# Strided sparse attention with a multiplicative FFN: batch 0's strided V issued from ScalarE's queue

## The chip, the cores and the metric

The kernel runs on one core of one Trainium2 chip. A core has a matrix engine (TensorE, PE in the profile), three engines for elementwise work (VectorE, DVE; ScalarE, ACT; GpSimd, POOL) and SyncE (SP), which here only issues DMA transfers. Each engine works off its own list of instructions in order and waits for others by semaphores. A DMA transfer is issued by an engine's instruction and carried out by the core's 16 DMA engines. The metric is the device time of one execution in microseconds (us).

## What is computed

Attention over 8 batches of 8 heads, 576 tokens and head dimension 64, in which the first four heads see the last 32 tokens only and the other four see every 32nd token, followed by a feed-forward network whose two first products are multiplied with each other.

```python
def _attn_ref(q, k, v):
    B, H, S, D = q.shape                      # 8, 8, 576, 64
    stride = 32
    scores = 1.0 / np.sqrt(D) * np.matmul(q, k.transpose(0, 1, 3, 2))
    rel = pos[:, None] - pos[None, :]
    mask_local = (rel >= 0) & (rel < stride)
    mask_strided = (rel >= 0) & (pos[None, :] % stride == pos[:, None] % stride)
    ...
    attn = softmax(np.where(masks, scores, -1e9))
    return np.matmul(attn, v)

def _moe_ref(x, w1, w2, w3, w_out):           # 4608 tokens, 512, 1024
    return ((x @ w1) * (x @ w2) @ w3) @ w_out
```

## The kernel before

Scores are computed for pairs of heads, four pairs a batch: pairs 0 and 1 (heads 0 to 3) are local, pairs 2 and 3 (heads 4 to 7) strided. For each pair PE transposes q and k, multiplies them, ScalarE takes the exponential, PE multiplies by V, VectorE divides by the sum, PE transposes the result into `xT`, and from there the feed-forward products follow (`ab_parts`, lines 632 to 684). The products w3 and w_out are folded into one matrix on the way (`fold_tr`, `fold_mm`).

Batches 0 and 1 have a scheme of their own (the functions named `ah_...`, lines 393 to 553). Batch 0 is what the core does while the weights are still coming, and its order on PE is written out by hand in `stream` (lines 832 to 884): every PE instruction is kept in the order in which the program emits it (`pe`, line 75). The first three units of `stream` are `ah_Ti(p0, 0)` (transposes of q for pair 0, and a ScalarE copy into `qT`), `both(p0)` (the mask's bias into PSUM) and `ah_Ti(p0, 1)` (the same for k, with a VectorE copy into `kT`). The fourth is `ah_R(0)`, which transposes q and k of the last 64 tokens and copies them into `qT` (ScalarE) and `kT` (VectorE), line 438.

Loads are emitted first, in lines 929 to 945, and all are issued by SyncE in that order: q and k of heads 0 to 3 (`load_qk(0, 0)`), the last 64 tokens of both (`load_rest`), q and k of heads 4 to 7 (`load_qk(0, 1)`), local V in four transfers of 96 x 6 pieces of 256 bytes (`load_vL`, line 231), strided V in two (`load_vN`, lines 238 and 240: 512 KB in pieces of 1,024 bytes and 64 KB in pieces of 256), eight transfers for w1 and w2 (`load_w12`, line 190), then w3, w_out and batch 1. Each lands as float32 in a staging tile, of which there are nine in a ring (`stgp`, line 64), and is cast to float16, mostly by GpSimd (the helper at line 91). The first batch's tiles fill the ring exactly, so the first weight tile waits for the cast of the first q, and so on round the ring; the seventh and eighth weights and the first w3 take the places of the second local V and of the two of strided V.

GpSimd's order at the start is: masks, cast of q (heads 0 to 3), cast of q and k (heads 4 to 7), then for each pair of local V a cast (line 232) and a copy that shifts rows (line 233), then two casts and a small one for strided V (lines 242 and 244), then the weights.

`behind(ins)` (line 80) puts the instructions emitted in its block behind `ins` on the same engine, without a semaphore. `setup` is a dictionary of such instructions. Where nothing of the kind is said, the tool that builds the program chooses an engine's order from the order of emission.

Of the kernel before, what the change touches and what calls it, by code (L numbers as in the profile page):

```python
# [14 lines left out]
def _ap(t: bass.AP, off_add, dims):  # L15
    return bass.AP(tensor=t.tensor, offset=t.offset + off_add, ap=dims)
# [3 lines left out]
def kernel(  # L20
# [11 lines left out]
    nc = tc.nc  # L32
    B, H, S, D = q.shape
# [3 lines left out]
    P = 128  # L37
# [10 lines left out]
    LQ, LT = 96, 6  # L48
    XW, XN, YW = 126, 4, 72
    XC = XW * XN  # L50
    NM = 512
# [8 lines left out]
    NW, NC, NQ = 144, 4, 640  # L60
# [14 lines left out]
    def pe(ins):  # L75
        return tc.keep_in_program_order(ins)

    setup = {}

    def behind(ins):  # L80
        return tc.issue_after(ins.ins) if ins is not None else nullcontext()
# [4 lines left out]
    def copy(eng, out, in_):  # L86
        if eng == "a":
            return nc.scalar.copy(out=out, in_=in_)  # L88
        elif eng == "v":
            return nc.vector.tensor_copy(out=out, in_=in_)  # L90
        return nc.gpsimd.tensor_copy(out=out, in_=in_)  # L91
# [25 lines left out]
    for m, lo, n, w in ((8, 208, 18, P), (32, 352, 2, 64), (7, 0, 18, XW), (4, P, 18, YW)):  # L117
        sel = tmp[0:m, NW + lo:NW + lo + n * m]
        nc.vector.tensor_copy(out=sel.rearrange("r (t a) -> r t a", a=m),
                              in_=_ap(id16, 0, [[id16.ap[0][0], m], [0, n], [1, m]]))  # L120
        pe(nc.tensor.matmul(mps[0:w, lo:lo + n * m], sel[:, 0:w], sel, start=True, stop=True))
    for i in range(1, LT):
# [7 lines left out]
                          in_=_ap(maskN, 0, [[maskN.ap[0][0], P], [0, NC - 1], [1, NW]]))  # L130
    nc.vector.tensor_copy(out=idw[:, P:2 * P - 32], in_=id16[:, 0:P - 32])
    biasL = tmp[:, S:2 * S]
    for bias, mask in ((biasL, maskL), (biasN, maskN)):
# [5 lines left out]
                                       in_=_ap(maskX, 0, [[maskX.ap[0][0], XW], [0, XN - 1], [1, XW]]))  # L139
# [44 lines left out]
    def load_w12(g):  # L184
        cs = bass.ds(g * 512, 512)
        for wd, wh in ((moe_w1, w1h), (moe_w2, w2h)):
            src = wd.rearrange("(c p) n -> p c n", p=P)
            for c in range(0, KM, 2):
                st = stgp.tile([P, 2, 512], FP32, tag="stg")
                nc.sync.dma_start(st, src[:, c:c + 2, cs])  # L190
                copy("p", wh[:, c:c + 2, cs], st)
# [4 lines left out]
    def load(b, out, in_):  # L196
        ins = nc.sync.dma_start(out, in_)  # L197
        if b > AHEAD + 1:
            pe(ins)


    def load_qk(b, grp, engs="pp"):
        for nm, ten, eng in (("q", q, engs[0]), ("k", k, engs[1])):
            st = stgp.tile([P, 4, 4, D], FP32, tag="stg")
            load(b, st.rearrange("p h c d -> p h (c d)"),
                 ten[b, 4 * grp:4 * grp + 4, 0:NM].rearrange("h (p c) d -> p h (c d)", c=4))
            t = qkp.tile([P, 4, 4, D], FP16, tag=f"{nm}{grp}")
            with behind(setup["p"] if b == 0 and grp == 0 else None):
                ins = copy(eng, t, st.rearrange("p h c d -> p c h d"))
            if b == 1:  # L210
                pe(ins)
            x16[(b, nm, grp)] = t
# [12 lines left out]
    def load_vL(b, hps=(0, 1)):  # L225
        vt = v16L[b % 2]
        for hp in hps:
            hs = slice(2 * hp, 2 * hp + 2)
            st = stgp.tile([P, 2, LT, D], FP32, tag="stg")
            for h in range(2):  # L230
                load(b, st[0:LQ, h], v[b, 2 * hp + h].rearrange("(t p) d -> p t d", p=LQ))
            nc.gpsimd.tensor_copy(out=vt[0:LQ, hs, :, 0:D], in_=st[0:LQ])  # L232
            copy("p", vt[LQ:P, hs, 0:LT - 1, 0:D], vt[0:32, hs, 1:LT, 0:D])

    def load_vN(b):
        vt = v16X[b % 2]
        st = stgp.tile([P, 4, 4 * D], FP32, tag="stg")
        nc.sync.dma_start(st, v[b, 4:8, 0:NM].rearrange("h (p c) d -> p h (c d)", c=4))
        sy = stgp.tile([64, 4, D], FP32, tag="stg", name="sy")
        nc.sync.dma_start(sy, v[b, 4:8, NM:S].rearrange("h r d -> r h d"))  # L240
        for hs in (slice(0, 2), slice(2, 4)):
            nc.gpsimd.tensor_copy(out=vt[:, hs, 0:NC, 0:D], in_=st[:, hs].rearrange("p h (c d) -> p h c d", c=4))
            if hs.start == 0:
                nc.gpsimd.tensor_copy(out=vt[0:64, :, NC, 0:D], in_=sy)

    def load_vX(b):
        vt = v16X[b % 2]
# [19 lines left out]
    for b in range(B):  # L267
        for hp in range(4):
            s = Pair()
# [133 lines left out]
    def ah_T1c(s, i, dst):  # L403
        t = (qT, kT)[i]
        eng = "av"[i]
        if s.local:
            copy(eng, t[:, s.hp, 0:NM].rearrange("x (p c) -> x p c", c=4),
                 dst.rearrange("x (c p) -> x p c", c=4))
        elif i:
            copy(eng, t[:, s.hp, 0:NM], dst)  # L410
        else:
            copy(eng, t[:, s.hp].rearrange("x (c w) -> x c w", w=NW)[:, :, 0:P],
                 dst.rearrange("x (c p) -> x c p", c=4))

    def ah_Ti(s, i):
        ah_T1c(s, i, ah_T1(s, i))

    def ah_T(s):
        if s.b:
            ps = psM.tile([P, 2, NM], FP16, tag="m", name="tps")  # L420
            pst = [ah_T1(s, i, ps[:, i]) for i in range(2)]
        else:
            pst = [ah_T1(s, i) for i in range(2)]
        for i in range(2):
            ah_T1c(s, i, pst[i])

    def ah_R(b):
        if b:
            ps = psB.tile([P, 2, NB], FP32, tag="big", name="rps").bitcast(FP16)[:, 0]
        else:  # L430
            ps = psM.tile([P, 1024], FP16, tag="m", name="rps")
        pvs = [ps[:, 256 * i:256 * i + 256].rearrange("x (g a w) -> x g a w", g=2, a=2) for i in range(2)]
        src = x16[(b, "r")]
        for g in range(4):
            pe(nc.tensor.transpose(pvs[g // 2][:, g % 2].rearrange("x a w -> x (a w)"),
                                   src[:, 2 * g:2 * g + 2].rearrange("p h d -> p (h d)"), id16))
        for i, t in enumerate((qT, kT)):
            copy("av"[i], t[:, 0:2, NM:S], pvs[0][:, :, i])
        copy("v", kT[:, 2:4, NM:S], pvs[1][:, :, 1])

        def tail():
            copy("a" if b else "v", qT[:, 2:4].rearrange("x g (c w) -> x g c w", w=NW)[:, :, :, P:NW],
                 pvs[1][:, :, 0].rearrange("x g (j c) -> x g c j", c=4))

        return tail
# [344 lines left out]
    stream = []  # L790
# [31 lines left out]
    def ah_Tw(s, i, n):  # L822
        ps = psF.tile([P, 2 * NM], FP16, tag="f", name="tps")
        ah_T1(s, i, ps[:, 0:NM])
        warm(ps, n)
        ah_T1c(s, i, ps[:, 0:NM])
# [7 lines left out]
    add(both, p0)  # L834
    add(ah_Ti, p0, 1)
    add(lambda: rest0.append(ah_R(0)))
    add(ah_S0, p0, (0,))
    add(ah_T, p1)
# [48 lines left out]
    for p, s in enumerate(pairs):  # L887
        b, i = divmod(p, 4)
# [18 lines left out]
    pos = [0]  # L907
# [22 lines left out]
    load_rest(0, "v")  # L930
    load_qk(0, 1)
    load_vL(0)
    load_vN(0)
    load_w12(0)
    load_w12(1)
# [6 lines left out]
    load_rest(1)  # L942
    load_qk(1, 1)
    load_vL(1)
    load_vN(1)

    while pos[0] < batch_end[0]:
# [32 lines left out]
    def scores(s):  # L980
        both(s)
        ah_S0(s, (0, 1))

    plan = ((15, ah_T, p4), (16, lambda: ah_R(1)()), (17, ah_T, p5), (17, ah_S, p4), (19, ah_S, p5),
            (20, ah_T, p6), (20, late_homes), (21, ah_PV, p4, 0), (22, scores, p6), (22, ah_T, p7), (22, ah_PV, p4, 1),
            (23, ah_PV, p5, 0), (24, scores, p7), (24, ah_PV, p5, 1), (24, ph_T2, p4), (25, ph_TS, None, p8),
            (26, ph_T2, p5), (26, ah_PV, p6, 0), (27, ah_PV, p6, 1))
    for i, u in enumerate(units[:-1], 1):
        u()
        for x in plan:  # L990
            if x[0] == i:
                x[1](*x[2:])
    load_vL(2)
    load_qk(2, 1)
    load_vX(2)
# [66 lines left out]
```

## Time and profile before

| | us |
|---|---|
| median of 3 runs | 271.12 (270.52 to 271.79) |
| profiled execution | 269.93 |
| its span, first to last instruction | 268.2 |
| PE busy | 257.8 |
| VectorE, ScalarE, GpSimd busy | 156.2, 140.3, 99.0 |
| DMA queue of SyncE, share of 16 engines over the span | 50.3% |

The profile is of one execution. Times in its views count from the start of the span. The page gives busy times and costly groups for the whole span; the timeline gives an engine's instructions in order (start, duration, engine, line, operation, tiles written and read, shapes, count, and in brackets the idle time before and what ended it); the windows give busy times and DMA rates of chosen stretches. A line such as L91 can be a helper's: the tiles tell which copy it is. `SPq` and `ACTq` mark issues by an engine's sequencer, which count as no busy time. How long a transfer takes from issue to landing stands in the DMA view.

DMA in stretches of the start (share of the 16 DMA engines' time, GB/s):

| us | share | GB/s |
|---|---|---|
| 8 to 9 | 1.08 | 372 |
| 9 to 10 | 1.23 | 301 |
| 10 to 11 | 0.89 | 204 |
| 11 to 12 | 0.94 | 154 |
| 12 to 13 | 0.71 | 129 |
| 13 to 14 | 1.07 | 369 |

### The profile page before, as it was taken

Reading aid. Unit: us, or ns where it says so; the run is one execution under the profiler, and the core shown is the slowest. Engines: PE = TensorE matmul, PEld = TensorE weight load, DVE = VectorE, ACT = ScalarE, POOL = GpSimd, SP = SyncE. Lnnn points to the kernel's source line nnn. Section 1 sums busy time; section 2 is a strip of 40 time slices with the busy share of each in tenths; the row PEclk is TensorE's granted clock in tenths of the full one; section 3 lists DMA queues with packets and bytes.
Section 4 is the critical chain, followed back from the end, with each engine's and each line's share of the span. In section 5 each row is a group of like instructions: output and inputs, shape, how many; then the busy total and the mean of one; then the engine's idle time right before and its main releaser. Section 6 shows DMA issues by size and latency. Waiting matters only on the chain.

```text
span 268.2 us, 6827 instructions
## 1 busy us (share of the span) xinstructions
PE 257.8 (96%) x2703; PEld 136.4 (51%) x2703; DVE 156.2 (58%) x373; ACT 140.3 (52%) x300; POOL 99.0 (37%) x119
## 2 busy tenths in 40 slices
PE   2999999999999999999999999999999999999993
PEld 1664464565555555555555555555555544444442
DVE  6573533555678766867776777667866752322420
ACT  1774334677566666555556465555466544324331
POOL 5576886778347206511840185038200000000000
PEclk9999999999999999999999999999999999999998
DMA  7999999988597569336923973397330022013013
GB/s 222 260 343 368 409 420 327 257 249 229 174 320 210 181 202 260 116 119 207 291 74 120 268 222 104 123 275 213 100 120 0 2 78 81 0 41 115 2 39 120
DMA packets 61101, 48.69 MB, mean 182 GB/s; under 512 B 31804, under 2 KB 52492, under 8 KB 61068
## 3 DMA queue, kind: packets, MB, share of 16 engines
q1 hardware_dynamic: 57036, 40.97, 50.3%
q10 hardware_dynamic: 4032, 7.28, 7.2%
q8 instruction: 21, 0.34, 0.5%
q14 instruction: 12, 0.10, 0.1%
HBM read 38.80 MB, written 9.44 MB: 180 GB/s over the span
## 4 chain that ended last, share of the span: by engine, by line
PE 85%; DMA 9%; SPq 3%; POOL 1%; issue 0%; ACT 0%; DVE 0%; POOLq 0%
PE ops L719 28%; PE bps L676 21%; PE aps L667 21%; DMA st<-in_moe_w_dram 8%; PE sps L389 3%; SPq L197 3%; PE t2a L586 2%; PE pt L301 2%; PE sps L352 2%; DMA st<-in_v_dram 2%; PE tps L399 1%; PE trp L777 1%; PE sps L480 1%; PE t L560 1%; PE ops L747 0%; PE rps L624 0%
## 5 line engine op out<-in xcount | busy, mean ns | idle before, releaser
L667 PE MATMUL aps<-xT,w1h 128*128 128x512 f16 (+1 forms) x288 | 73.5, 376 | 0.0
L676 PE MATMUL bps<-xT,w2h 128*128 128x512 f16 (+1 forms) x288 | 73.1, 376 | 0.0
L679 DVE TENSOR_TENSOR abt<-bps,asb 128x512 f16<-128x512 f32 (+1 forms) x72 | 48.5, 678 | 36.5 <-PE bps L676 35.0
L91 POOL CAST t<-st 128x1024 f16<-128x1024 f32 (+1 forms) x46 | 45.8, 1004 | 63.5 <-DMA st<-in_q_dram 43.3
L88 ACT COPY asb<-aps 128x512 f32<-128x512 f32 (+1 forms) x71 | 41.4, 584 | 51.2 <-PE aps L667 45.8
L719 PE MATMUL ops<-w,abt 128*128 128x512 f16 x280 | 67.1, 379 | 0.0
L676 PEld LDWEIGHTS <-w2h 128*128 128x128 f16 x288 | 27.1, 98 | 30.9 <-issue 0.7
L667 PEld LDWEIGHTS <-w1h 128*128 128x128 f16 x288 | 26.8, 98 | 28.6 <-issue 0.3
L719 PEld LDWEIGHTS <-abt 128*128 128x128 f16 x280 | 25.2, 98 | 26.2
L730 ACT COPY osb<-ops 128x512 f32<-128x512 f32 x35 | 21.0, 600 | 20.3 <-PE ops L719 19.9
L375 ACT ACTIVATE pte<-sps 128x1024 f16<-128x1024 f32 (+1 forms) x24 | 24.4, 1019 | 13.2 <-PE sps L352 12.8
L552 DVE TENSOR_TENSOR xqs<-sps,rcp 128x768 f16<-128x768 f32 (+1 forms) x24 | 21.4, 891 | 0.8
L364 DVE TENSOR_TENSOR ptm<-pte,maskE 128x1152 f16<-128x1152 f16 (+2 forms) x16 | 12.8, 801 | 7.1 <-ACT pte L375 6.7
L719 PE MATMUL ops<-woh,w3T 128*128 128x512 f16 x64 | 15.3, 380 | 0.0
L90 DVE COPY kT<-pt 128x512 f16<-128x512 f16 (+4 forms) x28 | 11.4, 417 | 6.5 <-ACT kT L88 4.8
L88 ACT COPY qT<-pt 128x224 f16<-128x224 f16 (+4 forms) x40 | 14.9, 422 | 0.2 <-PE pt L309 0.2
L364 DVE TENSOR_TENSOR ptm<-pte,maskX 126x1152 f16<-126x1152 f16 x12 | 10.4, 869 | 7.7 <-ACT pte L375 7.7
L232 POOL CAST v16L<-st 96x768 f16<-96x768 f32 x16 | 13.4, 836 | 3.4 <-DMA st<-in_v_dram 1.8
L260 POOL CAST v16X<-st 126x1024 f16<-126x1024 f32 x6 | 6.9, 1151 | 19.7 <-DMA st<-in_v_dram 19.7
L389 PEld LDWEIGHTS <-ptm 128*128 128x128 f16 (+1 forms) x264 | 11.1, 98 | 5.8 <-DVE ptm L364 0.8
L90 DVE COPY xT<-t2a 128x384 f16<-128x384 f16 (+1 forms) x22 | 8.5, 388 | 7.7 <-PE t2a L586 7.3
L91 POOL COPY v16L<-v16L 32x640 f16<-32x640 f16 x16 | 12.3, 768 | 1.0
(124 smaller groups left out, 274.8 us busy)
## 6 DMA issues: line engine op xcount, KB each, us to landing
st<-in_q_dram SPq DMA_DIRECT2D x16, 512.0 KB, 4.4
st<-in_k_dram SPq DMA_DIRECT2D x16, 512.0 KB, 5.5
st<-in_moe_w_dram SPq DMA_DIRECT2D x16, 512.0 KB, 10.0
out_dram<-osb ACTq DMA_DIRECT2D x27, 256.0 KB, 2.0
st<-in_v_dram SPq DMA_DIRECT2D x32, 144.0 KB
st<-in_v_dram SPq DMA_DIRECT2D x24, 112.0 KB, 2.5
st<-in_moe_w_out_dram SPq DMA_DIRECT2D x4, 512.0 KB, 11.0
out_dram<-osb SPq DMA_DIRECT2D x8, 256.0 KB, 3.9
```

Of the source, the lines that this page charges most:

```text
L88: return nc.scalar.copy(out=out, in_=in_)
L90: return nc.vector.tensor_copy(out=out, in_=in_)
L91: return nc.gpsimd.tensor_copy(out=out, in_=in_)
L364: nc.vector.tensor_mul(o.rearrange("p (a x) -> p a x", x=x), i.rearrange("p (a x) -> p a x", x=x), _ap(s.mask, lo, [[s.mask.ap[0][0], s.kr ...
L375: nc.scalar.activation(out=pv[0:kr, :, lo:hi], in_=src, func=AF.Exp, bias=0.0, scale=scale)
L389: pe(nc.tensor.matmul(s.ps[:, h, c * 65:c * 65 + 65], s.ptm[0:s.kr, c0:c0 + P], s.v[0:s.kr, 2 * (s.hp % 2) + h, c, :], start=True, stop=True))
L552: nc.vector.tensor_mul(s.xqs[0:w, c0:c0 + l].rearrange("p i h d -> p h i d"), xv[:, :, :, 0:D], _ap(rcp, 0, [[rcp.ap[0][0], w], [LT, 2], [ ...
L667: pe(nc.tensor.matmul(st["a"][:, 0:nt], w1h[:, ci, bass.ds(jc * P, P)], xT[ci][:, tok], start=(ci == 0), stop=(ci == KM - 1)))
L676: pe(nc.tensor.matmul(st["b"][:, 0:nt], w2h[:, ci, bass.ds(jc * P, P)], xT[ci][:, tok], start=(ci == 0), stop=(ci == KM - 1)))
L679: nc.vector.tensor_mul(abts[tch][:, jc, skip:], st["b"][:, 0:nt], st["asb"][:, 0:nt])
L719: pe(nc.tensor.matmul(st["ps"], lhs(ci), rhs(ci), start=(ci == 0), stop=(ci == KF - 1)))
L730: nc.scalar.copy(out=osb, in_=ps)
```

## The change

Batch 0's two transfers of strided V are issued by ScalarE, behind its first copy of q (`setup["q"]`, set where that copy is made), and no longer by SyncE behind local V. ScalarE's copy of q for the last 64 tokens is put behind the second of them (`setup["y"]`). GpSimd's three casts of strided V are put behind the last copy of local V (`setup["h", 0]`). So that the first copy of q exists when `load_vN(0)` is emitted, the first three units of `stream` are emitted ahead of it. Batch 1 stays as it was.

```diff
-            copy("p", vt[LQ:P, hs, 0:LT - 1, 0:D], vt[0:32, hs, 1:LT, 0:D])
+            setup["h", b] = copy("p", vt[LQ:P, hs, 0:LT - 1, 0:D], vt[0:32, hs, 1:LT, 0:D])
 
     def load_vN(b):
         vt = v16X[b % 2]
+        eng = nc.sync if b else nc.scalar
         st = stgp.tile([P, 4, 4 * D], FP32, tag="stg")
-        nc.sync.dma_start(st, v[b, 4:8, 0:NM].rearrange("h (p c) d -> p h (c d)", c=4))
         sy = stgp.tile([64, 4, D], FP32, tag="stg", name="sy")
-        nc.sync.dma_start(sy, v[b, 4:8, NM:S].rearrange("h r d -> r h d"))
+        with behind(None if b else setup["q"]):
+            eng.dma_start(st, v[b, 4:8, 0:NM].rearrange("h (p c) d -> p h (c d)", c=4))
+        with behind(None if b else setup["q"]):
+            setup.setdefault("y", eng.dma_start(sy, v[b, 4:8, NM:S].rearrange("h r d -> r h d")))
         for hs in (slice(0, 2), slice(2, 4)):
-            nc.gpsimd.tensor_copy(out=vt[:, hs, 0:NC, 0:D], in_=st[:, hs].rearrange("p h (c d) -> p h c d", c=4))
+            with behind(None if b else setup["h", b]):
+                nc.gpsimd.tensor_copy(out=vt[:, hs, 0:NC, 0:D], in_=st[:, hs].rearrange("p h (c d) -> p h c d", c=4))
             if hs.start == 0:
-                nc.gpsimd.tensor_copy(out=vt[0:64, :, NC, 0:D], in_=sy)
+                with behind(None if b else setup["h", b]):
+                    nc.gpsimd.tensor_copy(out=vt[0:64, :, NC, 0:D], in_=sy)
...
         if s.local:
-            copy(eng, t[:, s.hp, 0:NM].rearrange("x (p c) -> x p c", c=4),
-                 dst.rearrange("x (c p) -> x p c", c=4))
+            ins = copy(eng, t[:, s.hp, 0:NM].rearrange("x (p c) -> x p c", c=4),
+                       dst.rearrange("x (c p) -> x p c", c=4))
+            if i == 0:
+                setup.setdefault("q", ins)
...
         for i, t in enumerate((qT, kT)):
-            copy("av"[i], t[:, 0:2, NM:S], pvs[0][:, :, i])
+            with behind(None if i or b else setup["y"]):
+                copy("av"[i], t[:, 0:2, NM:S], pvs[0][:, :, i])
...
     load_vL(0)
+    while pos[0] < 3:
+        stream[pos[0]]()
+        pos[0] += 1
     load_vN(0)
     load_w12(0)
```

## The prediction

> **What bounds the kernel now.** I read the page first, for which engine carries the span and which chain ended last.
>
> ```profile
> span 268.2 us, 6827 instructions
> PE 257.8 (96%) x2703; PEld 136.4 (51%) x2703; DVE 156.2 (58%) x373; ACT 140.3 (52%) x300; POOL 99.0 (37%) x119
> ```
>
> TensorE is busy for 257.8 of 268.2 us. I then cut the span into stretches: from 20 us to 35 us PE is busy 15.0 of 15.0 us, from 35 to 40 us 4.94 of 5, from 60 to 200 us 139.9 of 140. So behind about 20 us PE only works off its list, and whatever the start loses or gains goes to the end almost undiminished. Only the stretch from 7 us (first scores) to 20 us can be changed by this edit, so I laid the engines' timelines of that stretch side by side. SyncE's queue first:
>
> ```profile
> 3.97 1.22 SPq L197 DMA_DIRECT2D st<-in_k_dram  x1
> 5.23 4.92 SPq L197 DMA_DIRECT2D st<-in_v_dram  x4
> 10.19 0.82 SPq L238 DMA_DIRECT2D st<-in_v_dram  x1
> 11.06 0.60 SPq L240 DMA_DIRECT2D sy<-in_v_dram  x1
> 11.77 5.21 SPq L190 DMA_DIRECT2D st<-in_moe_w_dram  x8
> ```
>
> Start and duration of each issue. The two that move are those at 10.19 and 11.06; in front of them are four of local V, behind them the weights. Now ScalarE, GpSimd and TensorE:
>
> ```profile
> 7.65 0.58 ACT L88 COPY qT<-tps 128x512 f16<-128x512 f16 x1
> 9.32 0.27 ACT L88 COPY qT<-rps 128x128 f16<-128x128 f16 x1 [1.09 <-PE rps L435]
> 9.83 0.70 ACT L505 ACTIVATE ptm<-sps 128x640 f16<-128x640 f32 x1 [0.24 <-PE sps L480]
> ```
>
> ```profile
> 9.51 1.04 POOL L91 CAST t<-st 128x1024 f16<-128x1024 f32 x1 [3.42 <-DMA st<-in_q_dram]
> 10.83 1.04 POOL L91 CAST t<-st 128x1024 f16<-128x1024 f32 x1 [0.28 <-DMA st<-in_k_dram]
> 11.98 0.83 POOL L232 CAST v16L<-st 96x768 f16<-96x768 f32 x1
> 16.44 0.40 POOL L244 CAST v16X<-sy 64x256 f16<-64x256 f32 x1
> 17.52 1.04 POOL L91 CAST w1h<-st 128x1024 f16<-128x1024 f32 x1 [0.68 <-DMA st<-in_moe_w_dram]
> ```
>
> ```profile
> 12.24 0.84 PE L399 MATMUL tps<-idw,t 128*128 128x128 f16 x12
> 14.33 0.54 PE L537 MATMUL xpl<-v16L,ptm 128*128 128x65 f16 x12
> ```
>
> The reader is to see three things. ScalarE has a hole of 1.09 us behind its first copy of q. GpSimd waits for the second k (heads 4 to 7), which lands late, and from then on works without a pause until the strided V is done at 16.84. TensorE takes that k at 12.24, 0.37 us after its cast ended at 11.87. The last view is DMA between 3.3 and 5.1 us, where the last figure is issue to landing:
>
> ```profile
> st<-in_q_dram SPq DMA_DIRECT2D x1, 512.0 KB, 6.2
> st<-in_k_dram SPq DMA_DIRECT2D x1, 512.0 KB, 6.8
> ```
>
> The second q landed at 9.45 and the second k at 10.77, so they are 1.32 us apart. By the completion records, 15 of the 16 DMA engines had finished that k at 10.02 and one at 10.77; the same one is last in every transfer of the start. This engine, not the mean, sets each landing.
>
> **The change, part by part.**
>
> (a) *SyncE loses two issues.* The first weight issue can move from 11.77 to 10.19, 1.58 us earlier. But it lands 5.7 us after its issue (17.47), behind everything older, and the slowest DMA engine gets no less work. Worth nothing as long as that engine has no hole; GpSimd takes all eight of these weights as they land (0.2 to 1.2 us idle before each), and PE reads the first at 18.70, after its cast ends at 18.57. If the weights did land earlier, PE's only visible wait behind 20 us that hangs on them is 0.06 us at 36.3 (the idle part of 35 to 40 us). Bounds -0.2 (all of the 230 ns by which the matmul at 36.36 starts behind its predecessor's pace) and 0; I take -0.06.
>
> (b) *ScalarE gains two issues between its copies at 7.65 and 9.32, and the second copy is put behind them.* What is queued behind: that copy (q of the last 64 tokens, heads 0 to 3), then the first exp at 9.83, and from there ScalarE is busy nearly without a hole until 13.9. No such load on ScalarE's queue is in the trace. Nearest rows: 0.45 us for the same shape of load from SyncE's empty queue (at 0.80), 0.34 us for ScalarE's own stores, 0.82 and 0.60 us for these very two from SyncE's loaded queue. So 0.9 to 1.5 us for both with their gaps. The room: ScalarE's sequencer is free between 7.66 (the copy started) and 8.23 (it ended); the copy at 9.32 may slip 0.24 us before it moves the exp, so the room ends at 9.56. 1.33 to 1.90 us. It fits except at the worst of both (8.23 + 1.5 = 9.75, 0.2 late). I take 0; bounds 0 and +0.2, and a blocked queue is a rival below.
>
> (c) *The transfers start earlier and share the DMA engines.* The first packet came 1.12 us after the issue at 0.80 and 1.49 us after that at 10.19 (11.68, by the packet records). So they now begin between 7.66 + 1.12 = 8.78 and 8.23 + 1.49 = 9.72, while the second k is still on the slowest engine (its last packet starts at 10.42). If the two queues take turns there, each remaining packet of k waits for one of V: between 9.72 and 10.42 that is 0.70 us; from 8.78 on it is all of V's large transfer, of the same shape as k and thus 1.32 us. Bounds for k: 0 if V's packets came behind, 1.32 if all come before. Taking turns is nearest to one queue serving equal parts, so I take the middle of 0.70 and 1.32, 1.0 us. The cast of k then ends at 12.87, and PE, which reads a cast 0.05 us after it ends, has 0.32 us of slack at 12.24: **+0.68 us on PE**.
> The Trainium skill, "DMA: Bandwidth & Descriptors", section "Issuing engines are not separate DMA queues", speaks against the change: transfers started by different engines run on the same 16 DMA engines and interleave, and a second issuer saves only its issue time. By that rule the sum is this same loss for k and nothing for the weights; without it V would be free.
>
> (d) *GpSimd's order is pinned behind the local V casts.* It is the order that the trace has (11.98 to 15.25 local, 15.32 to 16.84 strided), so 0. Local V also lands later on the slowest engine, by V's 1.32 us: its last part for the first cast landed at 11.85, now about 13.2. The cast at 11.98 moves by 1.2, and so does the unbroken row behind it: first local V complete 13.59 to 14.8 (PE wants it at 14.33 + 0.68 = 15.0), strided V 16.84 to 18.05 (PE wants the last part at about 17.75 + 0.68 = 18.4), first weights 18.57 to 19.15 (PE: 18.70 + 0.68 = 19.4). All three are covered by PE's own delay, by 0.2 to 0.3 us. If that cover is gone, it costs up to 0.3 more.
>
> (e) *Emission of three stream units moves ahead of the loads.* They hold PE, ScalarE and VectorE work whose neighbours on each engine stay; 0.
>
> Sum: -0.06 + 0 + 0.68 + 0 + 0 = +0.62, so the span goes from 268.2 to 268.8 us. The profiled execution took 269.93 us, 1.7 more than its span, and the median of the runs is 271.12; on that scale the forecast is **271.7 us**. A measurement of this kernel tells about 0.5% (1.36 us) from no change, so the likeliest case counts as "within".
>
> **Rivals.**
>
> *ScalarE is held by SyncE's issues (slower).* SyncE issues its last local V from 8.46 to 10.15, 1.69 us where an empty queue takes 0.5. If ScalarE's issues have to wait likewise, at 1.69 + 1.24 us (the slowest local V, the slowest `sy`) from 7.66 they end at 10.6; if they wait until SyncE has done, at 10.15 + 1.47 = 11.6. Then the copy of 9.32 is 1.3 to 2.3 late, less 0.24 of slack: +1.1 to +2.1, 272.7 in the middle. It decides as soon as the issues end after 9.56. Against it, in the window around 87 us:
>
> ```profile
> 86.37 1.87 SPq L197 DMA_DIRECT2D st<-in_v_dram  x3
> 87.57 0.38 ACTq L734 DMA_DIRECT2D out_dram<-osb  x1
> ```
>
> ScalarE's store was issued amid three of SyncE's and took 0.38 instead of 0.34 us. Those queues were not full, though. The Trainium skill, "Perfetto Trace Analysis", section "DMA Instruction — HWDGE (DVE, Sync)", has the descriptor generator locked for one issuer at a time; by that the 11.6 above would hold, which the row at 87.57 does not bear out.
>
> *PE falls back to its slow pace.* The 128x128 transposes took 314 ns until 10.4 us and 219 after, 107 and 56 ns apart; PE had been working since 7.0. The page's granted clock shows 1.0 throughout. If a hole of 0.7 us at 12.3 sends it back for such a 3.4 us, that costs up to 3.4 x (1 - 56/107) = 1.6, less the waits it has anyway (0.6 us around 15, by the starts of its matmuls): +0.9 to +1.6 on top of 0.62, 273.0. Against it: it waits 0.24 us for ScalarE at 15.56 already and stays fast.
>
> *Not slower.* Between 10 and 13 us DMA moved 204, 154 and 129 GB/s in three stretches of 1 us, against 372 between 8 and 9, with a DMA share down to 0.71. If V's packets fill that dip and k keeps its place, k is not late and (a) gives up to -0.2: 271.0. It needs the slowest engine to serve the older queue first; then (c) is 0 to 0.3 and vanishes in PE's slack.
>
> *The change does not do what it says:* ScalarE's issue gets through only when SyncE's would have, and nothing moves: 271.1.
>
> **Chances.** Forecast 0.40, ScalarE held 0.20, slow pace 0.12, not slower 0.23, nothing 0.05. Slower by over 0.5% (beyond 272.5): most of the second and third and the forecast's upper tail, 0.14 + 0.11 + 0.06 = 0.31. Faster by over 0.5% only by something unseen: 0.07. Range 270.3 (not slower, with the runs' own spread of 0.6 below) to 273.7 (slow pace with its spread); the forecast alone: 271.0 to 272.4.
>
> **What would show it.** Two ScalarE issues between 7.66 and 9.56, ending before the copy at 9.32 (b); GpSimd's cast of the second k at about 11.8 instead of 10.83 and PE's twelve transposes at about 12.9 (c); the local V cast near 13.2 and no wait of PE for it (d); the weights landing where they did (a). If k's cast stays at 10.83, (c) is wrong and the time is 271.0; if the copy of 9.32 starts at 10.5 or later, the held queue is right; transposes of 314 ns after 12 us would show the slow pace.

## The result, and the profile after

| | before | changed |
|---|---|---|
| median of 9 runs each, us | 271.30 (270.52 to 272.54) | 273.22 (272.09 to 274.88) |
| profiled execution, us | 269.93 | 272.69 |
| its span, us | 268.2 | 271.0 |

The changed kernel takes 1.0061 times as long, interval 1.0036 to 1.0086: slower by some 1.7 us. It lies inside the range of 270.3 to 273.7, 1.5 us above the forecast of 271.7.

First the head of the profile's page, then SyncE's and ScalarE's timelines (start, duration) of the changed kernel:

```profile
span 271.0 us, 6827 instructions
PE 259.6 (96%) x2703; PEld 137.2 (51%) x2703; DVE 157.1 (58%) x373; ACT 140.2 (52%) x300; POOL 98.4 (36%) x119
```

```profile
4.81 4.79 SPq L197 DMA_DIRECT2D st<-in_v_dram  x4
9.72 7.53 SPq L190 DMA_DIRECT2D st<-in_moe_w_dram  x8
```

```profile
6.13 1.04 ACT L88 CAST t<-st 128x1024 f16<-128x1024 f32 x1 [4.05 <-DMA st<-in_k_dram]
6.36 0.48 ACTq L241 DMA_DIRECT2D st<-in_v_dram  x1
7.09 0.58 ACT L88 COPY qT<-tps 128x512 f16<-128x512 f16 x1
7.24 0.71 ACTq L243 DMA_DIRECT2D sy<-in_v_dram  x1
8.58 0.27 ACT L88 COPY qT<-rps 128x128 f16<-128x128 f16 x1 [0.91 <-PE rps L442]
9.39 0.70 ACT L513 ACTIVATE ptm<-sps 128x640 f16<-128x640 f32 x1 [0.55 <-PE sps L488]
```

The two issues did move: they take 0.48 and 0.71 us and end at 7.95, and the pinned copy at 8.58 waits for PE's transposes, not for them. The weights start at 9.72 instead of 11.77. The moved transfers' packets came much later than their issues: the first at 9.82. The DMA view (packets, MB, share of 16 engines' time) has ScalarE's queue, q10, not at all from 8 to 9.8 us, and from 9.8 to 10.4 us beside SyncE's q1:

```profile
q1 hardware_dynamic: 1231, 0.60, 114.4%
```

```profile
q10 hardware_dynamic: 130, 0.13, 62.3%
q1 hardware_dynamic: 313, 0.08, 57.6%
```

Now GpSimd and PE:

```profile
8.48 1.04 POOL L91 CAST t<-st 128x1024 f16<-128x1024 f32 x1 [2.83 <-DMA st<-in_q_dram]
10.37 1.04 POOL L91 CAST t<-st 128x1024 f16<-128x1024 f32 x1 [0.85 <-DMA st<-in_k_dram]
...
14.23 0.82 POOL L232 CAST v16L<-st 96x768 f16<-96x768 f32 x1 [1.23 <-DMA st<-in_v_dram]
...
17.37 2.01 POOL L91 CAST w1h<-st 128x1024 f16<-128x1024 f32 x2
```

```profile
10.25 0.34 PE L488 MATMUL sps<-qT,kT 64*128 64x96 f16 x4
11.24 0.24 PE L488 MATMUL sps<-qT,kT 64*128 64x64 f16 x2 [0.64 <-DVE kT L90]
11.40 0.61 PE L404 MATMUL tps<-idw,t 128*128 128x128 f16 x4
11.80 0.63 PE L828 MATMUL tps<-idw 128*128 128x128 f16 x4
...
13.93 0.99 PE L404 MATMUL tps<-idw,t 128*128 128x128 f16 x12
```

The second k is cast at 10.37, 0.46 us *earlier* than before, and PE takes it only at 13.93, 2.5 us after its cast has ended. Instead PE stands still at 10.6 for 0.64 us, waiting for VectorE. The same place in the kernel before has no wait, and what follows runs faster there:

```profile
10.58 0.29 PE L480 MATMUL sps<-qT,kT 64*128 64x96 f16 x6
10.80 0.40 PE L399 MATMUL tps<-idw,t 128*128 128x128 f16 x4
11.03 0.39 PE L820 MATMUL tps<-idw 128*128 128x128 f16 x4
```

What VectorE does there, before and then changed:

```profile
9.62 0.35 DVE L90 COPY kT<-rps 128x128 f16<-128x128 f16 x2 [0.34 <-ACT qT L88]
9.89 0.28 DVE L90 COPY qT<-rps 128x128 f16<-128x128 f16 x1
10.68 0.69 DVE L90 COPY kT<-tps 128x512 f16<-128x512 f16 x1 [0.51 <-PE tps L399]
```

```profile
10.36 0.69 DVE L90 COPY kT<-tps 128x512 f16<-128x512 f16 x1 [1.51 <-PE tps L404]
10.96 0.35 DVE L90 COPY kT<-rps 128x128 f16<-128x128 f16 x2
11.23 0.28 DVE L90 COPY qT<-rps 128x128 f16<-128x128 f16 x1
```

The order is turned round. The copies of the last 64 tokens of k (`kT<-rps`) could run at about 8.9, when ScalarE's copy of 8.58 has ended, but now stand behind the copy of pair 1's k (`kT<-tps`), which waits 1.51 us for PE's transposes. PE needs the last 64 tokens for the two matmuls at 11.24.

Matching the two traces matmul by matmul gives where the span's 2.76 us went. The changed kernel is 0.43 us ahead at its first transposes (its first q landed earlier), still 0.33 ahead at 10.25, and 0.56 behind at 11.24: a step of 0.88 for the wait. By 13.93 it is 1.69 behind, another 1.12 without any wait: PE there works at another pace. The groups of PE's instructions (busy us, mean ns of one, idle) show it; these are the transposes of one source line, in the changed kernel from 11.4 to 13.9 us and in the kernel before in the like stretch, from 10.8 to 13.1:

```profile
L828 PE MATMUL tps<-idw 128*128 128x128 f16 x4 | 0.6, 314 | 0.0
```

```profile
L820 PE MATMUL tps<-idw 128*128 128x128 f16 x8 | 0.8, 219 | 0.0
```

At 314 ns each PE is at the slow pace that it had until 10.40 us in the kernel before; in the changed one it lasts until 14.29. These moments are the starts of the first clock record in each trace, and the spacing of the 128x128 matmuls changes there from 107 to 56 ns. From 20 to 36 us the distance is 1.76. At 36 us PE catches up 0.23 (a wait is gone) and at about 110 us 0.19, which leaves 1.34, and between 110 and 195 us the distance grows by another 1.38, which the section on the hardware takes up.

So there are two suspects, VectorE's order and the slow pace, and the question is what made each, and whether the transfers themselves cost anything.

### The profile page after: what moved, and what is told of

Same layout as the page of the kernel before. It is cut to its first block, busy times and chain, and to the rows that moved or that the text cites. A ratio compares the mean times of both kernels' runs of the same rounds, so it can differ in the third digit from the quotient of the medians.

```text
span 271.0 us, 6827 instructions
## 1 busy us (share of the span) xinstructions
PE 259.6 (96%) x2703; PEld 137.2 (51%) x2703; DVE 157.1 (58%) x373; ACT 140.2 (52%) x300; POOL 98.4 (36%) x119
## 4 chain that ended last, share of the span: by engine, by line
PE 90%; DVE 5%; ACT 3%; issue 1%; ACTq 0%; DVEq 0%
PE ops L727 28%; PE aps L675 22%; PE bps L684 21%; PE sps L394 3%; PE pt L306 2%; PE t2a L594 2%; PE tps L404 2%; PE sps L357 2%; DVE ptm L369 2%; PE sps L500 2%; PE sps L488 1%; ACT pte L380 1%; PE t L568 1%; DVE abt L687 1%; PE xpl L545 1%
## 5 line engine op out<-in xcount | busy, mean ns | idle before, releaser
L380 ACT ACTIVATE pte<-sps 128x1024 f16<-128x1024 f32 (+1 forms) x24 | 24.4, 1018 | 13.2 <-PE sps L357 12.8
L369 DVE TENSOR_TENSOR ptm<-pte,maskX 126x1152 f16<-126x1152 f16 x12 | 11.9, 994 | 7.6 <-ACT pte L380 7.6
L90 DVE COPY kT<-pt 128x512 f16<-128x512 f16 (+4 forms) x28 | 11.4, 417 | 6.3 <-ACT kT L88 4.6
L232 POOL CAST v16L<-st 96x768 f16<-96x768 f32 x16 | 13.2, 824 | 3.9 <-DMA st<-in_v_dram 3.2
```

The lines of the kernel that those rows point to most:

```text
L369: nc.vector.tensor_mul(o.rearrange("p (a x) -> p a x", x=x), i.rearrange("p (a x) -> p a x", x=x), _ap(s.mask, lo, [[s.mask.ap[0][0], s.kr ...
L380: nc.scalar.activation(out=pv[0:kr, :, lo:hi], in_=src, func=AF.Exp, bias=0.0, scale=scale)
```

## The experiments

All ratios are to the kernel before, run beside them on the same chip. e1 to e4 share one set of such runs (median 270.98), e5 to e8 a second (272.21), and e9 and e10 a third (271.87).

**e1: the changed kernel with VectorE's order put back.** VectorE's copy of pair 1's k is pinned behind the last 64 tokens' copy of k.

```diff
-            ins = copy(eng, t[:, s.hp, 0:NM].rearrange("x (p c) -> x p c", c=4),
-                       dst.rearrange("x (c p) -> x p c", c=4))
+            with behind(setup["r", 0] if i and s is pairs[1] else None):
+                ins = copy(eng, t[:, s.hp, 0:NM].rearrange("x (p c) -> x p c", c=4),
+                           dst.rearrange("x (c p) -> x p c", c=4))
...
-        copy("v", kT[:, 2:4, NM:S], pvs[1][:, :, 1])
+        setup["r", b] = copy("v", kT[:, 2:4, NM:S], pvs[1][:, :, 1])
```

> The changed kernel with one pin more: VectorE's copy of k for pair 1 is put behind its copies of k for the last 64 tokens, as in the kernel before. Theory O (the loss comes from VectorE's order, which makes PE wait 0.64 us at 11.2 us and keeps it at its slow pace for one stretch of 3.4 us more): PE's last two 64x64 score matmuls of pair 0 no longer wait, its 128x128 transposes are 56 ns apart from about 10.4 us, and the time is that of the kernel before within 0.3% (271.0 to 271.6), if anything 0.2 us less for the earlier weights. Rival C (the loss comes from the two queues sharing the DMA engines and from ScalarE's issues): 272.7 to 273.5, as the changed kernel.

Measured: 271.54 us, ratio 1.0016 (0.9990 to 1.0042); the loss can't be seen any more. PE's timeline:

```profile
10.44 0.39 PE L489 MATMUL sps<-qT,kT 64*128 64x96 f16 x6
10.76 0.61 PE L404 MATMUL tps<-idw,t 128*128 128x128 f16 x4
```

The wait is gone (six matmuls in a row, the next at 10.76), though the pace stays slow until 14.14 and not, as expected, until about 10.4.

**e2: the kernel before with VectorE's order spoilt, no transfer moved.**

```diff
         for i, t in enumerate((qT, kT)):
-            copy("av"[i], t[:, 0:2, NM:S], pvs[0][:, :, i])
-        copy("v", kT[:, 2:4, NM:S], pvs[1][:, :, 1])
+            if i == 0 or b:
+                copy("av"[i], t[:, 0:2, NM:S], pvs[0][:, :, i])
+        if b:
+            copy("v", kT[:, 2:4, NM:S], pvs[1][:, :, 1])
...
+            if b == 0:
+                with behind(setup["k1"]):
+                    copy("v", kT[:, 0:2, NM:S], pvs[0][:, :, 1])
+                    copy("v", kT[:, 2:4, NM:S], pvs[1][:, :, 1])
```

(`setup["k1"]` is the copy of pair 1's k, set where that copy is made; the last four lines stand in the function that ends `ah_R`'s work, emitted later.)

> The kernel before with VectorE's order alone changed: the copies of k for the last 64 tokens are emitted later and put behind the copy of k for pair 1; all loads are issued by SyncE as before. Theory O: slower by 1.2 to 2.2 us (272.5 to 273.5), with PE waiting for VectorE's copy at about 11 us and its transposes 107 ns apart until about 13.8 us. Rival C: as before within 0.3%.

Measured: 273.18 us, ratio 1.0054 (1.0026 to 1.0082). With every load still on SyncE, the same order on VectorE brings the same wait of PE and the whole loss. VectorE's timeline, then PE's line for the two matmuls that wait:

```profile
10.38 0.69 DVE L90 COPY kT<-tps 128x512 f16<-128x512 f16 x1 [1.52 <-PE tps L399]
10.98 0.35 DVE L90 COPY kT<-rps 128x128 f16<-128x128 f16 x2
```

```profile
11.25 0.24 PE L488 MATMUL sps<-qT,kT 64*128 64x64 f16 x2 [0.64 <-DVE kT L90]
```

**e3: the changed kernel with PE kept at work in the hole.** Six matmuls on the identity, whose result nobody reads, ahead of the six score matmuls of which the last two wait.

```diff
+    add(lambda: warm(psF.tile([P, 2 * NM], FP16, tag="f", name="wps"), 6))
     add(ah_S0, p0, (1,))
```

> The changed kernel with six 128x128 matmuls into a PSUM tile that nobody reads, in front of the second group of pair 0's scores, where PE then waits 0.64 us. VectorE's order stays. If the slow pace hangs on how busy PE was in the stretch before, PE now reaches its fast pace at about 10.4 to 11 us, and 0.9 to 1.2 us of the loss are gone (272.0 to 272.4), while the wait itself (0.6 to 0.9 us) stays. If the pace has nothing to do with the hole: 273.2 or up to 0.3 more.

Measured: 271.65 us, ratio 1.0027 (0.9996 to 1.0057), against 1.0061 for the changed kernel as it is; in the profiled execution the pace switched at 10.96 instead of 14.29. VectorE's order is still there, and so is the delay: the six take 0.75 us from 10.44 on, and PE still waits 0.18 us in front of the two. About half of the loss thus looks to be pace and not the wait, though the two intervals overlap.

**e4: the changed kernel without the pin on ScalarE's copy.**

```diff
-            with behind(None if i or b else setup["y"]):
-                copy("av"[i], t[:, 0:2, NM:S], pvs[0][:, :, i])
+            copy("av"[i], t[:, 0:2, NM:S], pvs[0][:, :, i])
```

> The changed kernel without the pin that puts ScalarE's copy of q for the last 64 tokens behind its second issue. VectorE's order is then that of the kernel before, and ScalarE issues behind that copy, some 1.5 us later than in the changed kernel. Theory O: the time of the kernel before within 0.3% (271.0 to 271.6) as long as the two issues (0.5 and 0.7 us) delay the first exp by less than 0.5 us; with the exp later by 0.7 to 1.0, up to 272. Rival C: the transfers still share the engines, 272.5 or more.

Measured: 271.35 us, ratio 1.0009 (0.9984 to 1.0034). VectorE's order is that of the kernel before: the last 64 tokens of k are copied at 8.89, pair 1's k at 10.37.

```profile
8.89 0.36 DVE L90 COPY kT<-rps 128x128 f16<-128x128 f16 x2
10.37 0.69 DVE L90 COPY kT<-tps 128x512 f16<-128x512 f16 x1 [0.93 <-PE tps L404]
```

This names the cause of the new order. VectorE's copies of the last 64 tokens wait for ScalarE's copy of them (the row at 9.62 of the kernel before); that copy was pinned behind ScalarE's second issue; and with this pin the tool that builds the program puts VectorE's copies in the other order. How it chooses is not shown. The transfers are still issued by ScalarE here, though later, at 8.60 and 9.08, and cost nothing that can be measured.

**e5: the kernel before, unchanged, profiled again**, because its first profile might have shown a lucky pace.

> The kernel before once more, for a second profile of it. If the moment at which PE goes from 107 to 56 ns between 128x128 transposes differs from execution to execution, it is not at 10.4 us again but somewhere between 10.4 and 14.2 (the mended kernel had 14.1, though PE waited no more there than in the kernel before). If it is fixed by PE's list, it is at 10.4 plus or minus 0.4.

Measured: 271.03 us in one run. PE's timeline:

```profile
10.23 0.39 PE L480 MATMUL sps<-qT,kT 64*128 64x96 f16 x6
10.56 0.61 PE L399 MATMUL tps<-idw,t 128*128 128x128 f16 x4
10.96 0.63 PE L820 MATMUL tps<-idw 128*128 128x128 f16 x4
```

The same program, the same order, no wait, and yet slow until 14.95 here and until 10.40 in its first profile; the spans are 269.3 and 268.2. So the moment of the switch belongs to the execution and not to the kernel alone, and the first profile of the kernel before is of a quick execution, by 1.1 us of span against this one. Against this second profile the changed kernel loses 0.84 us at the wait, but its fast pace begins 0.66 us sooner (14.29 against 14.95), and from 17 to 60 us it is only 0.13 us behind. A pair of profiles shows the wait; what the change costs can be told from the medians alone.

**e6, e7, e8: kept warm from the start.** 33 matmuls of 128x128 on the identity, in PE's idle time of the first 6.7 us, in the kernel before (e6), in e1's kernel (e7) and in the changed one (e8). This is meant to bring the fast pace forward and to leave VectorE's order as the difference between e8 and e7.

```diff
+    wps = psF.tile([P, 512], FP32, tag="f", name="wps")
+    def prewarm(n):
+        for _ in range(n):
+            pe(nc.tensor.matmul(wps[:, 0:P], id16, id16, start=True, stop=True))
+    prewarm(20)
     # the masks' matmuls
...
+    prewarm(10)
...
     add(ah_Ti, p0, 0)
+    add(prewarm, 3)
```

> The kernel before with 33 matmuls of 128x128 on the identity into a PSUM tile that nobody reads: 20 in front of the mask's first matmul, 10 behind its last, 3 behind pair 0's transposes of q, all where PE waits. If PE's pace follows how busy it was in the 3.4 us before, it is fast from 5 to 8.5 us on in every execution: 0.5 to 1.5 us faster than the kernel before (269.5 to 270.5), and the spread of the runs, 2 to 3.5 us so far, shrinks. If the pace is set otherwise: no change within 0.2%.

> The changed kernel with VectorE's order mended, and the same 33 matmuls. With the pace out of the way, what the move to ScalarE's queue is worth by itself is its distance from the prewarmed kernel before: 0 within 0.2% if k and local V land in time, 0.3 to 1.0 us slower if PE at full pace now waits for the second k or for local V (the mechanism of the prediction's part (c) and (d)), 0.2 us faster if the earlier weights count.

> The changed kernel as it is, with VectorE's order that makes PE wait, and the same 33 matmuls. Its distance from the mended prewarmed kernel is the price of the wait alone: 0.6 to 0.9 us. If the wait costs only through the pace, 0 to 0.2 us.

| | median, us | ratio to before | slow pace until, us |
|---|---|---|---|
| e6, before | 270.42 | 0.9944 (0.9913 to 0.9975) | 9.47 |
| e7, changed, order mended | 269.47 | 0.9912 (0.9882 to 0.9942) | 10.13 |
| e8, changed | 270.19 | 0.9935 (0.9912 to 0.9958) | 7.67 |

The fast pace came later than the expected 5 to 8.5 us in e6 and e7, and the spread of e6's runs (269.16 to 272.74 us) did not shrink. e8 is 0.72 us above e7 in the medians, within the expected 0.6 to 0.9 us for VectorE's order alone; but the two intervals overlap, so this price is an estimate. Nor is e8 slower than e6 (270.19 against 270.42). PE's timelines of e8 and of e7 at the place:

```profile
9.55 0.26 PE L496 MATMUL sps<-qT,kT 64*128 64x96 f16 x4
10.53 0.20 PE L496 MATMUL sps<-qT,kT 64*128 64x64 f16 x2 [0.73 <-DVE kT L90]
10.67 0.40 PE L412 MATMUL tps<-idw,t 128*128 128x128 f16 x4
```

```profile
1.54 2.31 PE L121 MATMUL wps<-idw 128*128 128x128 f16 x20 [1.54 <-POOL idw masks.py:199]
...
10.39 0.40 PE L412 MATMUL tps<-idw,t 128*128 128x128 f16 x4
...
16.40 0.53 PE L554 MATMUL xpl<-v16L,ptm 128*128 128x65 f16 x12 [0.21 <-POOL v16L L91]
...
18.97 0.61 PE L684 MATMUL aps<-xT,w1h 128*128 128x512 f16 x2 [0.22 <-POOL w1h L91]
```

e7 has no wait at 10.39 but two small ones later, for local V and for the first weights, which land late and which a later PE would have covered. In this profiled pair the wait sets e8 back by 0.89 us against e7, yet at 20 us e8 is 0.39 us ahead, because e7 was slow for longer (10.13 against 7.67) and has its own two waits; so the pair does not confirm the 0.72. By its median e7 is the fastest kernel here. Against e6 its distance is 0.95 us, with intervals that overlap; in the profiled pair it doesn't come from the start, where e7 is 0.57 us *behind* e6 at 18.97, but for the most part from a wait of e6 for VectorE at 85 us (0.62). That moving the transfers is worth something at full pace is therefore indicated and not shown. Without the added matmuls nothing of it is to be seen (e1 and e10).

**e9, e10: the changed kernel and e1's kernel again, beside each other**, with no edit, because e1's distance to the changed kernel came from two sets of runs.

> The changed kernel once more, beside the mended one on the same chip. Slower than the kernel before by 0.4 to 0.8% as in its own runs; in the profile PE waits 0.64 us at 10.6 us as in the first one (the order is fixed), and becomes fast between 12 and 15 us (not fixed).

> The changed kernel with VectorE's order mended, once more. If the order is all of the loss, it is the kernel before within 0.25%, and faster than the changed kernel beside it by 0.3 to 0.6% (0.7 us of wait and up to 0.9 us of slow pace). If the queues have a share, it is slower than the kernel before by over 0.3%.

Measured: 272.83 us, ratio 1.0036 (1.0008 to 1.0065), and 271.30 us, ratio 0.9983 (0.9953 to 1.0012), so 1.53 us apart on one chip. e9's profile has the same wait once more:

```profile
11.95 0.23 PE L488 MATMUL sps<-qT,kT 64*128 64x64 f16 x2 [0.64 <-DVE kT L90]
```

It stayed slow until 17.38 (12 to 15 was expected), and e10 until 13.15. Beside the profile of the changed kernel, which is slow through the same stretch, e10 starts the four transposes behind the place of the wait at 10.58 instead of 11.40: 0.82 us for the wait at the slow pace. If 0.72 of the 1.53 us are the price of the order at full pace (e8 less e7, an estimate), some 0.8 are left for the pace. e3's step from 1.0061 to 1.0027, 0.9 us, is of the same size. How the loss divides between the two is thus indicated and not shown; that the order brings all of it on is shown by e1, e2, e4 and this pair.

## Why the prediction was right in time and wrong in its mechanism

The forecast was +0.6 us from a late k; the result is about +1.7 us, and PE waits for no k. That the time lies in the range is luck: 273.2 is beyond the 272.4 that the forecast alone reached, in the part of the range that stood for rivals, and the wait of PE that did come, for VectorE, was in none of them.

- **(a), SyncE's lost issues: right as to the issues.** The weights were issued 2 us earlier, and the first of them was cast at 17.37 instead of 17.52, now without a wait. PE's wait near 36.36 is gone, 0.23 us: the bound of -0.2, not the -0.06 taken. That the earlier weights did this is not shown, for e5, the kernel before again, has no such wait either: its PE arrives there at 37.77, 0.93 us after the cast has ended.
- **(b), ScalarE's issues at 0: right for the issues.** They started at 6.36 and 7.24, earlier than the 7.66 from which I counted: the first even before the copy that it stands behind (7.09), while the cast of 6.13 ran. They took 1.19 us, within my 0.9 to 1.5. The rival of the held queue falls with this row: SyncE was issuing without a pause from 4.81 to 9.60. The Trainium skill ("Perfetto Trace Analysis", "DMA Instruction — HWDGE (DVE, Sync)") has the descriptor generator locked for exclusive use; this trace shows no such delay, for ScalarE's issue of 6.36 to 6.84 overlaps SyncE's of 5.90 to 6.46 and 6.50 to 7.39. In e9 the second issue started only at 8.46 and ended at 9.15, still ahead of the copy behind it, which waited for PE.
- **(c), k later by 1.0 us and PE by 0.68: this is the term that failed.** It let V's packets begin 1.12 to 1.49 us after their issue. By the packet records the first came at 9.82, 3.46 us after the issue at 6.36, and k's last packet had started by 9.87, so the two hardly met; what held V's packets back is open. GpSimd's cast of k starts at 10.37. With SyncE alone it starts at 10.83, 11.10 (e5), 10.12 (e2) and 10.93 (e6): it varies by 1 us among kernels that issue alike. In the other six profiles in which ScalarE issues at 6.4 to 6.7 (e1, e3, e7 to e10) it starts between 9.89 (e10) and 11.54 (e9). In e9 V's packets and k's did overlap, from 9.31 to 10.87, but the load of the last 64 tokens, ahead of both, was late as well (cast at 8.53 instead of 7.31), and PE took that k only at 14.65 and had no wait for it. What the rival "not slower" described is what happened in the changed kernel: between 10 and 13 us DMA moved 374, 323 and 335 GB/s instead of 204, 154 and 129, so V's packets filled the dip, and k kept its place. The Trainium skill's rule that transfers of different issuers interleave on the same DMA engines ("DMA: Bandwidth & Descriptors", "Issuing engines are not separate DMA queues") shows behind k: from 9.82 to 12.43 us the large V transfer's packets ran beside SyncE's, and the second local V made GpSimd wait 1.23 us.
- **(d), local V later but covered: the cover right, the place wrong.** The first local V was cast at 11.40, not at the forecast 13.2 (11.98 before); the second came at 14.23 instead of 13.65, and PE did not wait for it in the changed kernel. That the cover is thin was right too: in e7, whose PE is earlier, local V costs 0.21 us and the first weights 0.22.
- **(e), "neighbours on each engine stay; 0": the step behind the result, and it was assumed, not derived.** I counted what is queued behind the pinned ScalarE copy on ScalarE alone. VectorE's copies wait for that copy, and their place in VectorE's list was nobody's to keep: only PE's order is written by hand. The new order costs about 1.5 us (e9 less e10), of which an estimated 0.72 at full pace (e8 less e7); e2 brings the loss about with no transfer moved, e1 and e4 remove it with the transfers moved.
- **The slow pace, a rival at 0.12 with +0.9 to +1.6, holds half.** A hole of 0.64 us did come, but at 10.6 and not at 12.3, for another reason, and PE did not fall back: it had not yet left the slow pace. Its cost is about 0.8 us by the estimate above. How much later the hole makes the switch is not settled, since the switch differs between executions of one kernel: it came between 10.40 and 14.95 us in the five profiles without the hole and without added matmuls, and at 14.29, 15.07 and 17.38 in the three with the hole.

One misjudgement more: I took the profiled execution's early switch (10.40 us) as the kernel's own, and so had PE fast where the hole was to come. It was one draw.

## What to carry to other kernels

An ordering pin on one engine can reorder another: after such an edit, list every engine's instructions in order around it, and pin those that must stay, above all the short copies for which the bounding engine waits. A gap on TensorE early in a kernel may cost more than its length, since it may prolong the slow pace (here a delay of 0.8 to 0.9 us at the gap and some 1.5 us in the medians; the difference is not pinned down). Idle TensorE time at the start can be filled with matmuls that nobody reads (0.56% here, interval 0.25 to 0.87). And before a gain or a loss is read from one profile against another, profile the old kernel twice.

## What the runs showed of the hardware that was not expected

TensorE's slow pace ended anywhere from 10.40 to 17.38 us in the eight profiled executions without added matmuls (10.40 and 14.95 in the kernel before, 14.29 and 17.38 in the changed one). The views of the granted clock do not show it: they read 1.0 from the start, although each trace holds no clock record ahead of the switch. The spacing of the 128x128 matmuls does, 107 ns before and 56 after. The Trainium skill, "TensorE: Matmul & The Clock Gate", section "What's actually happening", has a free-running activity window of about 3.4 us behind this and calls the count of slow matmuls variable from run to run; the trace agrees that it varies, by 4.55 us in one program and so by more than one such window.

VectorE's multiplication by the mask took longer where a cast of GpSimd was already running when it began. The changed kernel near 128 us, then the kernel before at the same work:

```profile
128.10 1.04 POOL L91 CAST t<-st 128x1024 f16<-128x1024 f32 x1 [11.31 <-PE bps L684]
128.13 1.62 DVE L369 TENSOR_TENSOR ptm<-pte,maskE 128x1152 f16<-128x1152 f16 x1 [0.72 <-ACT pte L380]
...
130.53 0.81 PE L675 MATMUL aps<-xT,w1h 128*128 128x512 f16 x3 [0.19 <-DVE abt L687]
```

```profile
126.78 1.20 DVE L364 TENSOR_TENSOR ptm<-pte,maskE 128x1152 f16<-128x1152 f16 x1 [0.72 <-ACT pte L375]
```

With nothing beside it, the same instruction takes 0.76 us (the median of its group). In the kernel before the cast ends 0.59 us after the multiplication has begun, here 1.01, and both times the multiplication ends 0.61 us after the cast; here PE then waits 0.19 us for VectorE. Where the multiplication began first, the cast paid: at 73.67 us of the changed kernel the multiplication took 0.75 us, and the cast begun at 73.80 took 1.52 instead of 1.04. Such waits make part of the 1.38 us that the profiled pair lost between 110 and 195 us. They come and go between executions, in e1, e2, e3, e6, e8, e9 and e10 as well, with and without the loss, so they are taken as no part of the change's price; no run took them away by themselves.
